# Requesting the inverse blocks of a pair's first chunk at the second step of a slot

## The chip, the cores and the metric

The kernel runs on one core of a Trainium2 chip. The metric is the device time of one execution in microseconds, as the median of several runs; lower is better.

## What is computed

The reference is a linear recurrence followed by a feed-forward layer. In the first part, for each of 4 batches and 8 heads, a 40 by 40 state runs over 768 time steps; in the second part the outputs of all heads are put side by side as 3072 tokens of 320 numbers.

```python
for t in range(S):                                   # per batch and head
    y[t] = einsum('d,de->e', r[t], state)
    Sa = einsum('de,e->d', state, a[t])
    state = state * w[t][None, :] - einsum('d,e->de', Sa, b[t]) + einsum('d,e->de', v[t], k[t])
h = maximum(x @ w_in, 0)                             # x: (3072, 320), w_in: (320, 2048)
out = (h * h) @ w_out                                # w_out: (2048, 320)
```

All of it is float32.

## The kernel before

The time axis is cut into six chunks of 128 steps, which with four batches gives 24 pieces of work, called chunks 0 to 23 here (`order`, line 138, runs over the batches fastest). Inside a chunk the recurrence is solved as a triangular system, so each chunk needs an inverse of a unit triangular matrix for every head. The matrices are made early (`early`, line 360), stored to DRAM (`kept_q`, `kept_m`, `kept_n`, `kept_d`), and inverted on GpSimd by forward substitution in eleven units of 1, 1, 2, 2, 2, 2, 2, 2, 4, 4 and 2 chunks (`solving`, line 456). `take` (line 442) loads a unit's matrices into `half_n`; the last instruction of `solving` writes the inverses to `kept_t`.

For units 0 to 7 (chunks 0 to 13, "fine" in the code) only the inverses of 32 by 32 diagonal blocks are computed on GpSimd. The generator `inverses` (line 495) puts them together to 64 by 64 inverses `T` in four stages, each ending at a `yield`:

1. the requests on the SyncE queue: two transfers of `blocks` from `kept_t` (line 508), one of `N` from `kept_n` (line 489), two of `joins`, a part of the tile `spares`, from `kept_m` (line 493);
2. a transpose of `blocks` on VectorE (line 515) and two scaled copies of `blocks` into `T` on ScalarE (line 517);
3. 16 small matmuls with `joins` on TensorE and two copies out of PSUM (line 527);
4. 16 small matmuls with `blocks` and two copies into `T` (line 534).

Chunks 0 to 6 are woven into an opening whose order is written out by hand. From chunk 7 on each chunk has a slot, `sorted_slot` (line 973), which interleaves four things in an order written out by hand: the chain of chunk i (`ch`: the triangular solve, the output, the state), the preparation of chunk i+1 (called j), the early part of one or two later chunks (`one`, `two`), and the feed-forward layer of earlier tokens (`second`). There is no scheduler: the order in which the code issues is the order on each engine's queue. `tick` runs at the end of each `step` and issues delayed stores.

The preparation of chunk j includes the four stages of `inverses` for j. Where chunk j has the same unit as chunk j-1 (chunks 9, 11, 13, the second of a pair) or its request stood in the opening (chunk 8), stage 1 has been issued before slot j-1 begins: `loads`, line 956, does it at the end of the slot before. These chunks are `early_join`. The first chunk of a pair, which among the slots with fine units is chunk 10 (slot 9) and chunk 12 (slot 11), is not.

The slot calls `join()`, which advances `inverses` by one stage, at two places for fine chunks (lines 999 and 1006), once more at line 1011 if the chunk is not `early_join`, and runs what is left at line 1021. So in slots 9 and 11 stage 1 stands at line 999, stage 2 at 1006, stage 3 at 1011 and stage 4 at 1021; in slots 7, 8, 10 and 12 stage 2 stands at 999, stage 3 at 1006 and stage 4 at 1021.

At line 992, `on(one)` starts the early part of a later chunk, which first requests that chunk's successor's w, b and a (`load_early`, line 149). At line 993 `fetch_next` requests r for chunk j+1; at line 1008 it requests v. The store of 128 output rows is issued by `make_quarter` two ticks after its copy (line 789). All of these are on the SyncE queue. The built program gives the transfers on this queue eight semaphores in turn, so that a request may have to wait until the one eight places ahead of it has landed.

Of the kernel before, what the change touches and what calls it, by code (L numbers as in the profile page):

```python
# [17 lines left out]
def kernel(  # L18
# [82 lines left out]
    def tick():  # L101
        for entry in line:
            entry[0] -= 1
        while line and line[0][0] <= 0:
            line.pop(0)[1]()
# [389 lines left out]
    def inverses(i, g, queue=nc.sync, own_n=True):  # L495
        bb, c = order[i]
        u = unit_of[i]
        kept = kept_t[u][:, i - units[u][0]]
        g["T"] = T = new("T", [128, H, HC], 2)
        if u >= FINE:  # L500
            for col in range(classes(u)):
                queue.dma_start(out=T[col::classes(u)], in_=kept[col].rearrange("h f j t -> (f j) h t"))
        else:


            blocks = new("blocks", [128, H, Q], 1)
            for col in range(classes(u)):
                queue.dma_start(out=blocks[col::classes(u)], in_=kept[col].rearrange("h f k j t -> (f k j) h t"))  # L508
        if own_n:
            arrive(i, g, queue)  # L510
        if u >= FINE:
            return
        yield
        upper_ = spare("turned", i)
        nc.vector.transpose(upper_.rearrange("p h t -> p (h t)"), blocks.rearrange("p h t -> p (h t)"))
        for n in range(2):
            nc.scalar.activation(T[:, :, n * Q:(n + 1) * Q], blocks, Act.Copy, scale=which[:, n:n + 1])
        yield
        small = lambda: psum(ps_w)[:, :H * Q].rearrange("p (h t) -> p h t", h=H)
        p_ = small()  # L520
        mv = spare("mv", i)
        ends_ = [(slice(half * HC, half * HC + Q), slice(half * HC + Q, (half + 1) * HC)) for half in range(2)]
        for h in range(H):
            for one, two in ends_:
                mm(p_[two, h], g["joins"][one, h], upper_[one, h], True)
        for one, two in ends_:
            nc.scalar.copy(mv[two], p_[two])
        yield
        p_ = small()
        for h in range(H):  # L530
            for one, two in ends_:
                mm(p_[one, h], mv[two, h], blocks[two, h], True)
        for one, two in ends_:
            nc.scalar.copy(T[one, :, Q:], p_[one])
        yield
# [61 lines left out]
    def begin(i, g):  # L597
        g["x"] = loaded.pop(i)
        g["up"], g["aT"] = g["dec"][:, UP], g["dec"][:, A_, :, :C]
# [206 lines left out]
    def run(gen):  # L806
        for _ in gen:
            tick()
# [13 lines left out]
    def prepare(i, g=None, apart=False, steps=0):  # L822
        gen = early(i, g, apart)
        for _ in range(steps):
            next(gen)
            yield
        if i + 1 < len(order) and i + 1 not in early_loaded:
            load_early(i + 1)
        yield from gen
# [63 lines left out]
    def begin_chain(j, n_=None):  # L893
        n_ = decays_of(j)
        n_["chain"] = chain(j, n_)
        next(n_["chain"])
# [54 lines left out]
    def fetch_next(i, *names):  # L951
        if i < len(order):
            to = ready[i]["x"] if "x" in ready.get(i, {}) else loaded.setdefault(i, {})
            to.update({nm: fetch(nm, {"k": k, "b": b, "r": r, "v": v}[nm], i) for nm in names if nm not in to})

    def loads(j):
        if j < len(order):
            n = ready.setdefault(j, {})
            n["dec"] = kept_here[j % 2]
            nc.sync.dma_start(out=n["dec"][:USED], in_=kept_e[j])  # L960
            fetch_next(j, "k", "b")
            if soon(j) and j > B:
                n["joining"] = inverses(j, n)
                next(n["joining"], None)

    def step(*what):
        for w_ in what:
            w_()
        tick()
# [3 lines left out]
    def sorted_slot(i, g, ch):  # L973
        j = i + 1
        more = j < len(order)
        n = ready.setdefault(j, {}) if more else None
        made = [prepare(m_, apart=True) for m_ in ahead.get(i, ())]
        one, two = (made + [iter(()), iter(())])[:2]
        if j in inversions:
            n["joining"] = inversions.pop(j)  # L980
        early_join = more and "joining" in n
        joining = n.pop("joining") if early_join else inverses(j, n) if more else iter(())
        fine = more and unit_of[j] < FINE
        join = on(joining)
        of = lambda fn: (lambda: fn(j, n)) if more else (lambda: None)

        if more and "x" in n:
            n.update(up=n["dec"][:, UP], aT=n["dec"][:, A_, :, :C])
        elif more:
            begin(j, n)  # L990
        step(second.make_quarter)
        step(of(turn_rv), on(one), on(one))
        fetch_next(j + 1, "r")
        step(second.make_quarter)
        step(on(ch), of(decay_state))
        step(of(make_rv), second.thirds)
        step(on(ch), on(one))
        if fine:
            join()
        step(second.whole)  # L1000
        step(on(ch))
        step(on(one), of(turn_k))
        step(on(one), on(ch), of(turn_down))
        step(on(ch), of(scale_kb))
        if fine:
            join()
        step(on(ch), of(make_a), second.thirds, on(one))
        fetch_next(j + 1, "v")
        step(of(turn_state), second.square, second.whole, on(two))
        if not early_join:  # L1010
            join()
        run(ch)
        if more:
            begin_chain(j, n)
        loads(j + 1)
        step(second.square, second.make_quarter, on(two), on(two))
        if i in ahead and len(ahead[i]) > 1:
            step(on(two), on(two))
        step(second.make_quarter, on(two))
        for gen in (one, two, joining):  # L1020
            run(gen)

    for i in range(LAID, len(order)):
        tc.no_sync_barrier()
        g = ready.pop(i)
        opening[0] = 0
        ch = g["chain"]
        done.update(ahead.get(i, ()))
        sorted_slot(i, g, ch)
        while unit < len(units) and all(m_ in done for m_ in range(len(order)) if unit_of[m_] == unit):  # L1030
            flush()
            take(unit, own)
            solve(unit)
            unit += 1
# [32 lines left out]
```

## Time and profile before

| | us |
|---|---|
| median of three runs | 962.63 |
| lowest, highest run | 957.42, 964.86 |
| the profiled execution | 964.61 |
| its span, first to last instruction | 962.8 |

| engine | busy us | share of the span |
|---|---|---|
| TensorE matmul | 912.0 | 95% |
| TensorE weight load | 723.9 | 75% |
| GpSimd | 531.3 | 55% |
| VectorE | 452.6 | 47% |
| ScalarE | 287.2 | 30% |

The profile shows one execution. Times in it count from the start of the span; the 1.8 us between the span and the execution's own time lie outside the first and the last instruction. TensorE is busy nearly all the time, so a change is felt where TensorE stands still or runs at a lower granted clock, and only there. The slots from chunk 7 on can be told apart by the first chain matmuls of a slot (`ps_c<-xr,T`); slot 9 reaches from 417.14 to 459.60 us by this mark, slot 11 from 493.88 to 528.44 us.

### The profile page before, as it was taken

What the parts mean: (1) busy time and instruction counts of PE and PEld (TensorE: products, weight loads), DVE (VectorE), ACT (ScalarE), POOL (GpSimd) and SP (SyncE); (2) the same over time, 40 slices, a digit from 0 to 9 for tenths busy, and PEclk for the clock granted to TensorE, in tenths of its full rate; (3) what the DMA queues carried; (4) which work ended last, traced back from release to release, by engine and by line L of the source; (5) the groups of instructions that cost most, each with busy time, mean ns of one, the idle gap of its engine ahead of it and who ended that gap; (6) DMA issues with size and microseconds to landing.
All of it is one profiled execution on the core that took longest, in us unless ns stands there. A gap on an engine that the chain in (4) does not pass through costs nothing.

```text
span 962.8 us, 22650 instructions
## 1 busy us (share of the span) xinstructions
PE 912.0 (95%) x9156; PEld 723.9 (75%) x9156; DVE 452.6 (47%) x1064; ACT 287.2 (30%) x735; POOL 531.3 (55%) x1001
## 2 busy tenths in 40 slices
PE   5978989789999999989999999999999999999998
PEld 4645656568787887877888888887888888887776
DVE  4516647687863455533654543644234323231111
ACT  3123234544432343333423322222222222222111
POOL 4788508356008686319999849999768860000000
PEclk8889888798899999998999999999999999999999
DMA  9589767776875677893655695515554253120000
GB/s 110 113 160 175 155 129 139 170 177 126 163 116 131 114 159 138 168 170 82 114 90 99 116 191 110 110 24 85 120 112 78 44 107 69 42 42 9 14 14 14
DMA packets 253222, 103.36 MB, mean 107 GB/s; under 512 B 234143, under 2 KB 240159, under 8 KB 251967
## 3 DMA queue, kind: packets, MB, share of 16 engines
q1 hardware_dynamic: 246869, 83.43, 48.1%
q0 software_dynamic: 3600, 16.25, 6.8%
q10 hardware_dynamic: 2650, 2.25, 0.9%
q8 instruction: 72, 1.18, 0.6%
q14 instruction: 31, 0.25, 0.1%
HBM read 69.00 MB, written 30.92 MB: 104 GB/s over the span
## 4 chain that ended last, share of the span: by engine, by line
PE 80%; DVE 8%; ACT 3%; POOL 2%; issue 2%; SPq 2%; DMA 2%; DVEq 0%; POOLq 0%; ACTq 0%
PE ps_f L87 40%; PE ps_w L87 16%; PE ps_c L87 13%; PE ps_w L331 5%; PE ps_f L264 3%; PE ps_c L666 1%; PE ps_c L593 1%; SPq L508 1%; POOL half_p L477 1%; POOL half_t L479 1%; PE ps_w L577 1%; DMA blocks<-kept_t 1%; SPq L146 1%; DVE w_out L291 1%; DVE RX L347 1%
## 5 line engine op out<-in xcount | busy, mean ns | idle before, releaser
L477 POOL TENSOR_TENSOR half_p<-half_n,half_t 128x126 f32<-128x126 f32 (+44 forms) x437 | 232.0, 531 | 78.5 <-DMA half_n<-kept_d 23.0
L479 POOL TENSOR_TENSOR half_t<-half_t,half_p 128x126 f32<-128x126 f32 (+44 forms) x437 | 249.0, 570 | 34.2
L87 PE MATMUL ps_f<-w_out,hid 128*128 128x320 f32 x768 | 218.7, 436 | 0.0
L87 PEld LDWEIGHTS ps_f<-w_out,hid 128*128 128x128 f32 x768 | 142.0, 190 | 54.0 <-issue 0.2
L87 PE MATMUL ps_f<-tokens,w_in 128*128 128x256 f32 x672 | 160.1, 393 | 0.0
L87 PEld LDWEIGHTS ps_f<-tokens,w_in 128*128 128x128 f32 x672 | 128.4, 196 | 19.8 <-issue 2.0
L764 DVE TENSOR_TENSOR hid<-hid 128x512 f32<-128x512 f32 x96 | 82.3, 895 | 50.1 <-ACT hid L757 49.8
L757 ACT ACTIVATE hid<-ps_f 128x512 f32<-128x512 f32 x84 | 50.0, 597 | 88.2 <-PE ps_f L87 88.1
L264 PE MATMUL ps_f<-ident 128*128 128x512 f32 (+2 forms) x148 | 71.9, 625 | 0.0
L347 DVE TENSOR_TENSOR RV<-ps_w,upper 128x512 f32<-128x512 f32 x48 | 30.9, 685 | 50.3 <-PE ps_w L87 50.0
L451 POOL DMA_DIRECT2D half_n<-kept_q x18 | 9.4, 528 | 79.6 <-DMA kept_q<-N 51.6
L692 DVE TENSOR_TENSOR tokens<-ps_c,dec 128x512 f32<-128x512 f32 x24 | 16.6, 690 | 78.0 <-PE ps_c L87 78.0
L372 DVE TENSOR_TENSOR_SCAN decay<-ps_w,ones 128x64 f32<-128x64 f32 x88 | 23.6, 268 | 59.6 <-PE ps_w L331 59.4
L87 PE MATMUL ps_f<-tokens,w_third 64*128 64x256 f32 x336 | 47.4, 392 | 2.5 <-ACT hid L757 2.5
L264 PEld LDWEIGHTS ps_f<-ident 128*128 128x128 f32 x148 | 29.3, 215 | 26.7 <-issue 25.7
L347 DVE TENSOR_TENSOR RX<-ps_w,upper 128x512 f32<-128x512 f32 x48 | 30.8, 683 | 37.2 <-PE ps_w L87 36.8
L543 DVE TENSOR_TENSOR kvT<-ps_w,dec 128x512 f32<-128x512 f32 x24 | 16.5, 687 | 62.9 <-ACT minus_x L653 35.3
L87 PEld LDWEIGHTS ps_c<-xr,T 64*64 64x64 f32 x768 | 28.7, 143 | 20.4 <-issue 16.8
L398 ACT COPY N<-ps_w 128x256 f32<-128x256 f32 x48 | 17.7, 368 | 80.2 <-PE ps_w L87 54.8
L565 DVE TENSOR_TENSOR f<-end,dec 128x4 f32<-128x4 f32 x20 | 7.0, 348 | 64.7 <-DMA dec<-kept_e 64.7
L555 ACT COPY rT<-ps_w 128x512 f32<-128x512 f32 x24 | 14.0, 585 | 77.6 <-PE ps_w L331 77.5
L87 PE MATMUL ps_c<-xr,T 64*64 64x40 f32 x768 | 34.8, 237 | 1.4 <-ACT xr L660 0.8
(146 smaller groups left out, 1429.5 us busy)
## 6 DMA issues: line engine op xcount, KB each, us to landing
dec<-kept_e SPq DMA_DIRECT2D x22, 633.8 KB
kept_e<-decay SPq DMA_DIRECT2D x19, 633.8 KB
in_w<-in_w_dram SPq DMA_DIRECT2D x24, 160.0 KB
in_b<-in_b_dram SPq DMA_DIRECT2D x24, 160.0 KB
in_ab<-in_a_dram SPq DMA_DIRECT2D x24, 160.0 KB
in_r<-in_r_dram SPq DMA_DIRECT2D x24, 160.0 KB
in_v<-in_v_dram SPq DMA_DIRECT2D x24, 160.0 KB
out_dram<-o SPq DMA_DIRECT2D x24, 160.0 KB
```

The source lines that it names most:

```text
L87: nc.tensor.matmul(o, l_, r_, start=start, stop=True, skip_group_check=True)
L264: nc.tensor.matmul(fill_bank[:, :n * 128], ident, ident.unsqueeze(1).to_broadcast([128, n, 128]), start=True, stop=True, skip_group_check= ...
L331: nc.tensor.transpose(p_[:, q * 128:(q + 1) * 128], pair(x_, q), ident)
L347: nc.vector.tensor_tensor(t_, p_, over4(upper), Alu.mult)
L372: nc.vector.tensor_tensor_scan(up[:, q, MID + 1:C + 1], wT[:, q, MID:], ones, 1.0, Alu.mult, Alu.mult)
L398: nc.scalar.copy(plain, p_[:, ::2].rearrange("s h (f t) -> s f h t", f=2))
L477: nc.gpsimd.tensor_tensor(p_, part[:, at:at + m_].unsqueeze(1).to_broadcast([128, n, m_]), t3[:, :n, s:s + 1].to_broadcast([128, n, m_]), ...
L479: nc.gpsimd.tensor_tensor(t3[:, :n, s + 1:], t3[:, :n, s + 1:], p_, Alu.subtract)
L543: nc.vector.tensor_tensor(kT, kT_, down[:, :, 1:C + 1], Alu.mult)
L692: nc.vector.tensor_tensor(t_, y_, g["up"][:, :, :C], Alu.mult)
L757: nc.scalar.activation(h_, p_.rearrange("p f t -> p (f t)"), Act.Relu)
L764: nc.vector.tensor_tensor(h_, h_, h_, Alu.mult)
```

## The change

For fine chunks that are not `early_join`, one more `join()` is called right after the slot's first step, and the one at line 1011 is left out for them.

```diff
         step(second.make_quarter)
+        if fine and not early_join:
+            join()
         step(of(turn_rv), on(one), on(one))
         fetch_next(j + 1, "r")
...
         step(of(turn_state), second.square, second.whole, on(two))
-        if not early_join:
+        if not early_join and not fine:
             join()
```

This holds for chunks 10 and 12, thus for slots 9 and 11. In these two, stage 1 moves ahead of the slot's second step: on the SyncE queue its five requests stand in front of the requests for w, b and a of a later chunk, the request for r and the store of the output. (The request for v stood behind them before as well.) Stage 2 moves from line 1006 to line 999, and stage 3 from 1011 to 1006. The number of instructions on each engine stays the same, and no other slot changes.

The order of the instructions after the change, in slots 9 and 11, against before:

- SyncE: `blocks` twice, `N`, `spares` twice, then w, b, a, r, the output's store; before: w, b, a, r, the store, then the five.
- VectorE: the transpose of `blocks` comes directly after the scans of a later chunk (lines 380, 381) and ahead of `kvT`, `bT` and the scaling of k and b; before it came after them, directly ahead of `RX`.
- ScalarE: the two copies of `blocks` into `T` come ahead of the two ReLU copies `hid` and of the copy `minus_x`; before they came after `xnT`.
- TensorE: the 16 matmuls with `joins` come ahead of the products for `RX`; before they came ahead of the chain's `ps_c<-RV`.

The first `blocks` request waits on one more thing: the buffer `blocks` exists once, so TensorE must have done the last stage of the chunk before, the matmuls `ps_w<-blocks,spares`.

## The prediction

> **What bounds the kernel now.** I read the busy shares first (TensorE 95%), then the chain of waits that ended last. From 257 us on the chain is nearly all TensorE; the largest break in it is in slot 9:
>
> ```profile
> 424.97 0.29 ACT minus_x L653
> 425.26 1.54 SPq L110
> ...
> 426.89 1.90 SPq L508
> ...
> 428.85 5.36 DMA blocks<-kept_t
> ...
> 434.30 0.45 DVE spares L515
> 434.74 0.59 DVE RX L347
> ...
> 435.38 2.67 PE ps_w L87 x16
> ```
>
> Columns: start, length, what. So TensorE at 435.38 waits for VectorE's `RX`, that for the transpose of `blocks`, that for the transfer, that for its issue. Then I cut the table of busy times by slot (8 to 13) and slot 9 by its stall (length, then busy times of PE, weight loads, DVE, ACT, POOL, the granted clock, DMA share, GB/s):
>
> ```profile
> 379.95:417.14 37.19, 36.75 (x441) 31.05 (x440) 20.84 (x63) 13.63 (x39) 12.13 (x33) 1.00 0.85 161
> 417.14:459.60 42.46, 38.07 (x414) 31.63 (x413) 16.34 (x39) 11.85 (x31) 28.63 (x42) 0.92 0.65 121
> 459.60:493.88 34.28, 34.28 (x414) 28.77 (x413) 20.62 (x42) 11.54 (x31) 32.11 (x28) 1.00 0.71 119
> 493.88:528.44 34.56, 34.56 (x413) 29.11 (x412) 18.04 (x39) 11.65 (x31) 32.34 (x29) 1.00 0.38 79
> 528.44:562.72 34.28, 34.28 (x414) 28.77 (x413) 17.13 (x43) 11.54 (x31) 26.52 (x40) 1.00 0.81 155
> ...
> 430.99:435.38 4.39, 0.01 (x1) 0.01 (x1) 1.08 (x3) 0.91 (x2) 3.37 (x10) 0.92 0.79 171
> 435.38:441.51 6.13, 6.13 (x27) 5.26 (x28) 3.31 (x5) 2.68 (x9) 5.50 (x9) 0.50 0.27 79
> ```
>
> Slot 9 has as many matmuls as slots 10 and 12 (414) and takes 8.18 us more than either. It stands still for 4.39 us, then runs 6.13 us at a clock of 0.50. Half of these 6.13 us is 3.07 us, to which come some 0.37 us already inside the idle stretch and the slower start (clock 0.92 there), and 0.28 us that slot 11, equal in form and undisturbed, also takes over 34.28: 4.39 + 3.07 + 0.28 = 7.74, the other 0.44 us I leave as rounding of modelled ends. The difference between whole slots, 8.18, is what I use.
>
> Why is `blocks` late? The SyncE queue:
>
> ```profile
> 417.19 0.58 SPq L146 DMA_DIRECT2D in_w<-in_w_dram  x1
> 417.86 0.64 SPq L146 DMA_DIRECT2D in_ab<-in_b_dram  x1
> 418.59 0.55 SPq L146 DMA_DIRECT2D in_ab<-in_a_dram  x1
> 419.23 0.71 SPq L146 DMA_DIRECT2D in_r<-in_r_dram  x1
> 420.03 6.77 SPq L110 DMA_DIRECT2D out_dram<-o  x1
> 426.89 3.21 SPq L508 DMA_DIRECT2D blocks<-kept_t  x2
> ...
> 418.59 1.03 POOL L451 DMA_DIRECT2D half_n<-kept_d  x2 [23.79 <-DMA kept_d<-N]
> ```
>
> The store of the output sits in issue for 6.77 us, though its input was copied at 417.67; in slot 11 the same store takes 0.36 us. At 418.59 GpSimd requests unit 8, two transfers of 768 KB. The trace's packet records give the rest: the 128 packets of 12288 bytes of these transfers start at 420.0 and the last ends by 429.7, about 1 us each; the SyncE queue's packets of 160 bytes start at 1350 per us from 419 to 420, at 16 to 17 per us from 420.5 to 423.5, about 580 come through between 423.75 and 425.25 (between GpSimd's two transfers), and then 12 to 18 per us until 427.75. Four loads of 1024 packets each had been put in front; a little over half was through at 420.25. So `blocks`, behind them, lands at 434.2. VectorE and ScalarE had waited 5.45 and 7.17 us for it.
>
> **What the Trainium skill says.** "DMA: Bandwidth & Descriptors", section on queues, rings and completion order: each DMA engine goes round robin, packet by packet, between the queues that have work. The trace agrees: with 16 engines and 1 us per large packet, one small packet between two large ones gives the 16 per us. "Perfetto Trace Analysis", section on the HWDGE DMA instruction: the issue's recorded window begins when its semaphores are satisfied and holds the generation of descriptors[...]. So the 6.77 us are a full buffer and not a wait for an engine; the "ACT minus_x" put in the chain ahead of it is a coincidence. "TensorE: Matmul & The Clock Gate", part on the clock gate: an idle window of about 3.4 us puts the array at half clock until it has been busy for another. The trace agrees: 4.39 us idle, then a clock of 0.50.
>
> **The change part by part.** It only moves instructions, in slots 9 and 11.
>
> *Slot 9, requests.* SyncE is free at 417.14, after the store of `kept_n`. The new wait, for TensorE's last read of `blocks`, is over: those matmuls ran at 410.70 to 411.4. The inverses of this unit were stored at 359.24, and the transfers eight places ahead had landed by 417.85, or, for the later ones, before their turn. With the issue times of slot 11's five (0.65, some 0.7, 0.62, 0.6, 0.6), they start at 417.19, 417.85, 418.5, 419.15 and 419.75. From issue to landing the two `blocks` transfers took 3.0 and 2.7 us in slot 11 (494.89 to 497.92, 495.59 to 498.33); hence 420.2 and 420.6. First packets came 1.3 us after issue, and 512 packets take 0.4 us at 1350 per us: those of the second end near 419.6, 0.4 us before the first large packet. `N` (64 packets) falls on the edge, the two `joins` transfers (512 packets) inside the stretch at 16 per us; the gap at 423.75 to 425.25 lets 580 through, so I put their landing at 425.5 to 426.
>
> *Slot 9, who waits.* VectorE reaches the transpose at 422.3, where it then has 3.81 us without work: 0.45 us, free. ScalarE is done with `xr` at 421.05 and with nothing until 422.31: the two copies, 0.91 us, fit if `blocks` lands by 421.4; up to 422.5 only `hid` would shift, and from 423.1 on the chain's `minus_x` and TensorE's transposes of it at 425.89. TensorE wants `joins` in front of the `RX` products, at 10.61 us into the slot as in slot 10 (470.21 - 459.60), so at 427.75: about 2 us of slack. Then slot 9 has the order of slot 10 and should take its 34.28 us: -8.18 us.
>
> *Slot 9, what is pushed back.* The loads of w, b, a, r and the store move back by five requests, most of them behind GpSimd's burst. The sum of the packets is unchanged, so all should be through at about 434 as before. In slot 9 itself none of them is read; r is transposed first at 456.04, w at 456.91, minus 8.2 at the new pace: 14 us of cover. If this cover were gone, TensorE would stop at the next slot's start for as long as r was late. Behind them stand the store of decays, the stores of N for unit 9, v, the moves of tokens and the next slot's decays. The moves wait for VectorE's `tokens` at 447, 439 at the new pace, so a queue that is empty by 437 costs nothing.
>
> *Slot 11.* Here the new wait bites: the last read of `blocks` in slot 10 is at 487.44 to 488.06, while SyncE is free for the next request at 484.3. It stands 3.7 us with w, b, a, r and the store behind it; before, the same 3.6 us went into issuing w (484.36, 3.58 us). `blocks` then lands near 491.5, and is wanted from 497.8. No large burst is near (DMA share 0.38). The slot becomes 34.28 instead of 34.56: -0.28 us, which might as well be zero.
>
> *Afterwards.* From slot 10 on TensorE had no idle time in slots 10 to 13, so nothing hides the gain, but GpSimd's solving keeps its times, and TensorE comes 8.4 us earlier. The stores of unit 8, 9 and 10's inverses land at 560.6, 698.0 and 792.6; the first reads of them are requested at 582.2, 698.0 (here the queue already waits) and 814.2. For unit 9 the transfer lands at 706.8 and is used at 721.1, 712.7 at the new pace: 6 us of slack remain. GpSimd's request for unit 9 at 554.97 would meet slot 13 from its start instead of the end of slot 12; the loads that it delayed there (a, issued over 10.19 us) are then ahead of it.
>
> Sum: -8.18 - 0.28 = -8.46. Against the profiled execution's own time, 964.61, that is 956.15; it lies 1.98 above the median, so at the median 962.63 - 8.46 = 954.2, or -0.88%. About 1% is what a measurement of this kernel can tell from no change (the three runs spread over 7.4 us), so even the full gain is just inside it.
>
> **The rivals.**
>
> *A, the stall goes wholly (0.60):* 954.2; with the spread of the runs, 950 to 957.5.
>
> *B, a shorter wait takes its place (0.22):* `joins` has only the gap in GpSimd's burst to get through. If an engine's share is not through then, it comes with the burst's end at 429 or so, and TensorE stands about 2 us ahead of the `RX` products, too short for the clock; if `blocks`' last packets are caught, ScalarE holds `minus_x` until 425.3 + 2.65 and TensorE stands another 2 us. For it: packets inside the burst at 16 per us. Against: 512 packets, and 580 came through. 2 to 4 us are lost: 956.2 to 958.2.
>
> *C, no gain to be seen (0.10):* the stall is only in this execution (the lowest run, 957.42, may have none), or GpSimd's fixed pace takes the gain back, unit 9 being the tightest. Against: 6 us of slack there. 959 to 963.
>
> *D, slower (0.08):* the two copies and the transpose now stand in front of `minus_x` on ScalarE and of `kvT` on VectorE. If the burst catches `blocks` and it lands with the rest at 434.2, the chain stops at 425.89 and resumes 2.65 us (copies, two `hid`, `minus_x`) after the landing, at 436.85: 10.96 us idle, then 3.4 to 6.8 us for the clock, against 8.18 won: 968.8 to 972.2. From a landing at 428 on it is slower than before. Against: 0.4 us of margin before the burst, and the gap.
>
> **How the numbers follow.** Predicted is A: 954.2. The range reaches from A's lower end, 949.5, over B to most of C, 962.0; D and a rest of A and C are left out. Faster by over 1% means under 953.0: nearly half of A, a little of B, 0.30. Slower by over 1% means over 972.3: the upper end of D and runs of it, 0.06. The rest, 0.64, is within 1%.
>
> **What would show it.** Right: in slot 9 five requests ahead of `in_w`, `blocks` landing near 420.5, no idle TensorE near 431, a clock of 1.00 throughout, a slot of 34.3 us; slot 11 within 0.3 us; all later slots as long as before. The store of the output may still sit long in issue, now unnoticed. Wrong: an idle TensorE ahead of the `RX` products (B), ahead of `ps_c<-ident,minus_x` (D), or at slot 18's `ps_c<-xr,T` (C).

## The result, and the profile after

| | us |
|---|---|
| after, median of 20 runs | 958.21 (952.52 to 963.97) |
| before on the same chip, median of 20 runs | 961.64 (956.35 to 966.83) |
| ratio, 95% interval | 0.9966 [0.9948, 0.9984] |
| the profiled execution after | 959.58, span 957.7 |
| the profiled execution before | 964.61, span 962.8 |

The change gains 3.4 us at the median, where 8.46 were predicted. So less than half of the expected gain came. Measured twice more on other chips the same kernel gave 0.9918 [0.9893, 0.9944] and 0.9952 [0.9933, 0.9971]. How much the stall differs between executions of the same kernel is shown below.

First the table by slots for the kernel after, in the columns of before: slots 8, 9, 10 and 11, then the stall in slot 9 and the stretch at a lower clock that follows it.

```profile
380.56:417.75 37.19, 36.74 (x441) 31.06 (x441) 20.85 (x63) 13.75 (x39) 12.43 (x34) 1.00 0.88 166
417.75:454.71 36.96, 36.20 (x414) 30.19 (x413) 15.87 (x39) 11.55 (x31) 26.45 (x39) 0.95 0.74 135
454.71:488.98 34.27, 34.27 (x413) 28.76 (x412) 19.78 (x43) 11.55 (x31) 32.05 (x29) 1.00 0.64 115
488.98:523.26 34.28, 34.28 (x414) 28.76 (x413) 18.77 (x40) 11.55 (x31) 32.08 (x29) 1.00 0.49 85
...
428.43:429.13 0.70, 0.00 (x0) 0.03 (x1) 0.70 (x3) 0.00 (x0) 0.29 (x1) 1.00 1.37 93
431.90:435.30 3.40, 3.40 (x28) 2.96 (x24) 3.40 (x6) 0.00 (x0) 3.01 (x6) 0.51 0.86 254
```

Slot 9 fell from 42.46 to 36.96 us, not to 34.28. What is left over 34.28 is 2.68 us: 0.70 us in which TensorE has nothing to do, half of 3.40 us at half clock (1.7 us), and some 0.28 us that are not told apart. Slot 11 went from 34.56 to 34.28. All other slots from 7 on kept their lengths to 0.04 us; what lies ahead of slot 9 took 0.61 us longer in this execution. So 0.61 - 5.50 - 0.29 is the -5.2 us between the two profiled spans.

The SyncE queue of the kernel after (start, length, what), and below it GpSimd's request of unit 8 from the same view of its own queue:

```profile
416.60 1.37 SPq L508 DMA_DIRECT2D blocks<-kept_t  x2
418.02 0.62 SPq L489 DMA_DIRECT2D N<-kept_n  x1
418.69 1.25 SPq L493 DMA_DIRECT2D spares<-kept_m  x2
419.98 0.65 SPq L146 DMA_DIRECT2D in_w<-in_w_dram  x1
...
422.79 5.60 SPq L146 DMA_DIRECT2D in_ab<-in_a_dram  x1
...
429.76 0.87 SPq L110 DMA_DIRECT2D out_dram<-o  x1
```

```profile
418.12 1.04 POOL L451 DMA_DIRECT2D half_n<-kept_d  x2 [22.33 <-DMA kept_n<-N]
```

The `blocks` requests are out before GpSimd's burst and, by the trace's landing times, are in at 419.03 and 419.62. The two `spares` requests (that is `joins`) go out at 418.69 and 419.33 and land at 429.00 and 429.36, ten microseconds later. The long issue has moved from the output's store (6.77 us before) to the load of a (5.60 us). (The view puts GpSimd's request down to the store of `kept_n`. That store landed at 418.28, after the request; the last store of `kept_d`, which the request reads, landed at 417.39.)

What that does to TensorE, in its order of time (in brackets: idle before, and what ended it; the trace counts 32 instructions for the 16 matmuls with `joins`):

```profile
427.37 1.06 PE L87 MATMUL ps_c<-rT,sd 128*128 128x128 f32 x8
429.13 0.96 PE L87 MATMUL ps_w<-spares 32*32 32x32 f32 x32 [0.70 <-DMA spares<-kept_m]
...
431.91 1.88 PE L87 MATMUL ps_f<-tokens,w_third 64*128 64x256 f32 x8
433.58 1.92 PE L87 MATMUL ps_w<-decay,bT 40*128 40x128 f32 x16
```

and the chain of waits of this stretch, which before ran through `blocks`:

```profile
418.69 0.59 SPq L493
...
419.33 10.03 DMA spares<-kept_m
...
429.40 2.68 PE ps_w L87 x62
```

Followed back from TensorE, the chain goes to the transfer of `joins`, and from there along the SyncE queue and over ScalarE's making of `N` to a load of decays (`dec<-kept_e`, 405.16 to 411.46). The stall of before was not removed wholly: a shorter wait took its place, and the clock fell although the wait was short.

### The profile page after: what moved, and what is told of

Its sections match the earlier page's. It is cut to its first block, busy times and chain, and to the rows that moved or that the text cites. A ratio compares the mean times of both kernels' runs of the same rounds, so it can differ in the third digit from the quotient of the medians.

```text
span 957.7 us, 22644 instructions
## 1 busy us (share of the span) xinstructions
PE 913.9 (95%) x9156; PEld 725.4 (76%) x9156; DVE 451.0 (47%) x1064; ACT 287.4 (30%) x735; POOL 531.9 (56%) x1001
## 4 chain that ended last, share of the span: by engine, by line
PE 72%; DMA 4%; DVE 2%; ACT 2%; SPq 1%; issue 0%; ACTq 0%; DVEq 0%
PE ps_f L87 40%; PE ps_w L87 13%; PE ps_c L87 12%; PE ps_w L331 4%; DMA dec<-kept_e 2%; DMA spares<-kept_m 2%; PE ps_c L593 1%; PE ps_c L666 1%; PE ps_w L577 1%; DMA hid<-in_moe_w_out_dram 1%; ACT N L401 0%; SPq L508 0%; DMA kept_t<-half_t 0%; SPq L146 0%; SPq L110 0%
## 5 line engine op out<-in xcount | busy, mean ns | idle before, releaser
L87 PEld LDWEIGHTS ps_f<-tokens,w_third 64*128 64x128 f32 x336 | 31.0, 192 | 6.5 <-ACT hid L757 3.7
```

What stands on the lines that cost most here:

```text
L87: nc.tensor.matmul(o, l_, r_, start=start, stop=True, skip_group_check=True)
```

## The experiments

My theory after this reading: what is left is the wait of stage 3 (the 16 matmuls with `joins`) for a transfer that only lands with the end of GpSimd's burst; the early requests themselves are good. Rivals: the early stage 2 costs on VectorE and ScalarE; `N` in front of `joins` is what uses up the gap in the burst; the rest is the position of the burst in that execution.

**late_use: the requests early, the use where it was.** Stage 1 stays at the slot's second step, stages 2 to 4 go back to their places of before (the edit is shown against the changed kernel, from its line 1000 on).

```diff
-        if fine:
+        if fine and early_join:
             join()
...
-        if not early_join and not fine:
+        if not early_join:
             join()
```

> The changed kernel's order on the SyncE queue, with stages 2 to 4 left where the kernel before had them. Theory 1 (what is left of the stall is the joins transfers caught in GpSimd's burst, wanted too early by the moved stage 3): blocks lands near 419.6 us, ahead of the transpose at 428.8; joins lands near 429 and is wanted some 18.7 us into the slot, near 436; TensorE doesn't stop, no half clock, slot 9 takes 34.6 us instead of 37.0 (changed) and 42.5 (before), slot 11 34.6: some 2.1 us faster than the changed kernel, 5.5 us and more below the kernel before (0.994). Rival (the early request delays what stands behind it, r and the store, and that costs): slot 9 stays at 37 us or above, or slot 10 grows over 34.3, and the time stays at that of the changed kernel (0.9966).

953.57 us, ratio 0.9894 [0.9870, 0.9919], a larger gain than the 0.994 expected. Slot 9, and the matmuls with `joins` in it:

```profile
413.20:447.76 34.56, 34.56 (x413) 29.11 (x412) 15.69 (x38) 11.66 (x31) 24.08 (x37) 1.00 0.82 144
```

```profile
431.90 0.69 PE L87 MATMUL ps_w<-spares 32*32 32x32 f32 x32
```

The `joins` transfers land at 424.62 and 424.92, 10.5 and 10.2 us after their issue, as late as in the changed kernel. But they are wanted only 18.7 us into the slot instead of 10.7, so 7 us are to spare: no idle time, a clock of 1.00. A second measurement of the same kernel on another chip:

> The kernel with the requests at the slot's second step and the use of blocks and joins where it was before, once more, beside stage3_late on one chip. If its gain (0.989 in the first measurement) belongs to the kernel: 0.987 to 0.992 again, slot 9 at 34.3 to 34.6 us. If that was a lucky position of GpSimd's burst (it came 0.17 us into the slot there): slot 9 of 36 us or more here wherever the burst comes 1 us or more into the slot.

954.48 us, ratio 0.9924 [0.9897, 0.9951], just outside the expected 0.987 to 0.992; slot 9 took 34.57 us again. GpSimd's request came 0.23 us into the slot there, so this run did not test the kernel against a late burst; the next one did.

**stage3_late: only stage 3 put back.** The changed kernel, with stage 2 left early.

```diff
         step(on(ch), of(scale_kb))
-        if fine:
+        if fine and early_join:
             join()
...
-        if not early_join and not fine:
+        if not early_join:
             join()
```

> The changed kernel with one difference: the 16 matmuls with joins (stage 3) stand where they stood before the change, after the output and the state's parts, in slots 9 and 11; the requests at the slot's second step and the early stage 2 (transpose and copies of blocks) stay. My theory: what is left of the stall in the changed kernel is the wait of these 16 matmuls alone, for joins that land near 429 to 429.7 with the end of GpSimd's burst. Used later, they find joins there: TensorE has no idle time in slot 9, the slot takes 34.3 to 34.6 us, and the ratio to before is 0.989 to 0.991. Rival: the early stage 2 costs as well (VectorE's transpose ahead of kvT, ScalarE's copies ahead of minus_x); then slot 9 stays at 36 us or more and the ratio at 0.993 or above, as in the changed kernel.

954.90 us, ratio 0.9919 [0.9894, 0.9943]: the slot as expected, the ratio a little above the 0.989 to 0.991 named and under the 0.993 of the rival.

```profile
415.39:449.96 34.57, 34.57 (x413) 29.12 (x412) 15.70 (x38) 11.65 (x31) 22.69 (x35) 1.00 0.80 146
```

```profile
434.10 0.69 PE L87 MATMUL ps_w<-spares 32*32 32x32 f32 x32
```

Here GpSimd's request came 1.86 us into the slot, nearly as late as in the worst run of the changed kernel below, `joins` landed at 428.31 and 428.62, and TensorE still never waited, since it wanted them at 434.10. This is the cleanest test: same requests, same early transpose and copies, only the 16 matmuls later, and the remaining stall is gone. The early stage 2 costs nothing in this slot; the early stage 3 is what meets the burst.

**joins_first: the burst turned on `blocks`.** The changed kernel with the order `joins`, `blocks`, `N` in stage 1.

```diff
-            if unit_of[i] < FINE:
+            if unit_of[i] < FINE and "joins" not in g:
...
+            if i in (10, 12):
+                g["joins"] = spare("joins", i)
+                for half in range(2):
+                    queue.dma_start(out=g["joins"][half * HC:half * HC + Q], in_=kept_m[i][half, :, :, Q:])
```

> The changed kernel with the order of the five requests turned for chunks 10 and 12: joins twice, blocks twice, N last. Theory 1: joins issued at 416.6 lands near 419, blocks at 418 to 418.6 lands near 420.5, just ahead of the burst or with its tail in it; N lands at 430, but nobody reads it before slot 10. If blocks is in time, slot 9 takes 34.3 us, 2.7 us less than in the changed kernel, ratio to before about 0.993. If the tail of blocks is caught, ScalarE holds minus_x, and TensorE stops at the transposes of minus_x for up to 2 us: slot 9 at 36 to 38. Rival (not the joins but something else held TensorE at 429): slot 9 stays at 37.0 with the idle time at the same place.

960.40 us, ratio 0.9981 [0.9963, 0.9999]; slot 9 took 42.08 us, nearly as long as before and longer than the 36 to 38 us expected for a `blocks` caught by the burst. `joins` landed at 414.50 and 415.23, the second `blocks` transfer at 425.10, 10.7 us after issue. TensorE then stands where the prediction's slower rival put it, at the transposes of `minus_x`, held on ScalarE behind the copies of `blocks`:

```profile
427.43 1.21 PE L670 MATMUL ps_c<-ident,minus_x 128*128 128x128 f32 x4 [5.43 <-ACT minus_x L657]
```

So the mechanism of that rival exists. Here it was worth 5.43 us of idle time and 6.8 us at half clock, of which 2.2 us fell into the idle time. In the changed kernel `blocks` had landed by 419.62 in each of its three profiled executions, so it did not happen.

**joins_mid: `N` behind `joins`.** Order `blocks`, `joins`, `N`.

```diff
-            queue.dma_start(out=g["N"], in_=kept_n[i])
+            if i not in (10, 12):
+                queue.dma_start(out=g["N"], in_=kept_n[i])
...
+            if i in (10, 12):
+                queue.dma_start(out=g["N"], in_=kept_n[i])
```

> The changed kernel with N asked for last: blocks twice, joins twice, N, for chunks 10 and 12. Refined theory 1: in the changed kernel the 64 packets of 2048 bytes of N stood ahead of joins and used up the gap between GpSimd's two transfers, so that joins came only with the burst's end. With N last, the 512 packets of 128 bytes of joins pass in the gap (some 580 small packets did in the kernel before): joins lands 3 to 4 us earlier, about 6.5 us after its issue instead of 10.3, TensorE does not stop, slot 9 takes 34.3 us, the ratio to before is near 0.991. Rival (the gap is too short for joins whatever stands ahead of it): joins lands with the burst's end again, slot 9 stays between 34.8 and 37.

957.27 us, ratio 0.9931 [0.9913, 0.9950]; slot 9 took 39.64 us, above what either theory or rival had allowed. The theory that `N` alone kept `joins` from the gap fell:

```profile
424.75 0.24 PE L87 MATMUL ps_w<-spares 32*32 32x32 f32 x2
426.96 1.03 PE L87 MATMUL ps_w<-spares 32*32 32x32 f32 x30 [1.96 <-DMA spares<-kept_m]
```

Two matmuls run at 424.75, the other 30 wait for the second transfer, which landed at 426.91 with the burst's end. By the packet records exactly the 256 packets of the first transfer came through until the gap closed, and none of the second.

**after_again and after_third: the changed kernel once more**, on two other chips.

> The changed kernel once more, for a second profile and for times beside the three others. Theory 1: slot 9 again at about 37.0 us with an idle TensorE of 0.5 to 2 us ahead of the joins matmuls, ratio to before near 0.9966. Rival (the length of the stall varies by some us from run to run, which would bring 3.4 us in the medians against 5.0 in the profiled executions): slot 9 anywhere from 35 to 40 us.

> The changed kernel a third time. Theory 1: slot 9 between 34.8 and 38 us, set by where the end of the burst falls against the place of the joins matmuls at 10.6 us into the slot, and by whether the wait brings a stretch of half clock (3.4 us, costing 1.7); ratio to before between 0.992 and 0.9966. Rival: slot 9 always near one value, and the two ratios measured so far differ by something else.

The ratios are 0.9918 and 0.9952, given above. Slot 9 of after_again and its matmuls with `joins`; then the same of after_third:

```profile
418.29:453.13 34.84, 34.52 (x414) 28.88 (x413) 15.86 (x38) 11.53 (x31) 24.24 (x37) 1.00 0.77 138
```

```profile
429.29 0.88 PE L87 MATMUL ps_w<-spares 32*32 32x32 f32 x32 [0.32 <-DVE decay L388]
```

```profile
415.85:456.63 40.78, 37.76 (x413) 31.78 (x413) 16.39 (x38) 11.54 (x31) 27.86 (x41) 0.92 0.71 128
```

```profile
429.55 0.89 PE L87 MATMUL ps_w<-spares 32*32 32x32 f32 x32 [3.02 <-DMA spares<-kept_m]
```

(In after_again the first `joins` transfer landed at 429.15 and the scaling at L388 ended at 429.20, so there the two ended the wait together.) In the same program slot 9 took 34.84, 36.96 and 40.78 us; so the rival named for after_again, a stall that differs by some us between runs, holds, and after_third lies outside the 34.8 to 38 us expected. One number orders the three: how far into the slot GpSimd's request of unit 8 came.

| run | GpSimd's request, us into slot 9 | last `joins` lands, us into the slot | TensorE is free for it at | idle | at half clock | slot 9 |
|---|---|---|---|---|---|---|
| after_again | -0.61 | 11.14 | 10.68 | 0.32 | none | 34.84 |
| after | 0.37 | 11.61 | 10.68 | 0.70 | 3.4 | 36.96 |
| after_third | 1.94 | 13.85 | 10.68 | 3.02 | 6.8 | 40.78 |
| stage3_late | 1.86 | 13.23 | 18.71 | none | none | 34.57 |

The landing follows the request by 11.2 to 11.9 us in each. The request itself comes 0.73 or 0.74 us after the landing of the last store of `kept_d`, which it reads (417.39 and 418.12 in the kernel after, 416.94 and 417.68 in after_again, 417.05 and 417.79 in after_third), and those stores landed between 1.35 us ahead of the slot's start and 1.20 us behind it. What moves the stores against the slot from run to run was not pursued. Nor do these profiles explain the three ratios: each shows one execution, and 0.9966 goes with a slot of 36.96 us but 0.9952 with 40.78. Why the medians differ stays open.

**before_again: the kernel before once more**, for the size of its own stall.

> The kernel before once more, for a second profile. Theory 1: slot 9 near 42.5 us again, with blocks landing with the rest of the backlog. Rival: the stall differs by some us between runs of the same kernel; then slot 9 is under 40 us here, and this is why the medians differ less than the two profiled executions.

One run, 958.99 us beside a median of 963.56 for the others on that chip. Slot 9 took 41.75 us against 42.46, with 3.03 us idle, ended by VectorE's `RX`, and 6.8 us at half clock. So the stall of before is there in both profiled executions and nearly the same in length, as expected.

**burst_later: the burst away, the old order kept.** The kernel before, with unit 8's request moved to the SyncE queue at the end of slot 9 (the condition inside `all` is left out below).

```diff
-        while unit < len(units) and all(...):
+        while unit < len(units) and (unit != 8 or i >= 9) and all(...):
...
-            take(unit, own)
+            take(unit, [nc.sync] if unit == 8 else own)
```

> The kernel before, with GpSimd's request for unit 8 put on the SyncE queue at the end of slot 9, behind the requests for chunk 11; the rest in the order of before. Theory 1 (the burst, not the order of the requests, makes blocks late): w, b, a, r, the store and blocks all flow at full rate, blocks lands near 424, 4 us ahead of the transpose at 428.8, slot 9 takes 34.6 us although blocks is asked for late. Rival (the five requests ahead of blocks are enough to delay it): blocks lands after 429 and slot 9 takes 37 us or more. Unit 8's inverses come some 40 us later and are then late for chunk 14, so a new stall near 590 us is expected and the whole time says nothing.

982.94 us, one run. The total is not the point: GpSimd solves unit 8 late, so that TensorE waits 14.16 us for the inverses at the end of slot 13 (47.36 us) and begins slot 14 at half clock (37.51 us). Slot 9 is:

```profile
413.42:447.99 34.57, 34.57 (x414) 29.12 (x413) 14.47 (x38) 11.65 (x31) 0.00 (x0) 1.00 0.58 102
```

With requests in the order of before, `blocks` lands at 420.44 and 420.69, 3.1 and 2.7 us after issue, and slot 9 loses nothing. The place of the requests on the queue was never the fault by itself; the burst was. (GpSimd computes nothing in this slot either. That is not the cause: in slot 11 of the kernel before it was busy for 32.34 us, no burst ran, and the two transfers took 3.0 and 2.7 us.) The burst was taken away from the old order only; no run did so for the changed kernel.

**at_loads: the requests a slot earlier.** The kernel before, with stage 1 of chunks 10 and 12 issued at the end of the slot before, as for the other fine chunks; this makes them `early_join`, with the early use of stages 2 and 3.

```diff
-    soon = lambda i: i < 2 * B or unit_of[i - 1] == unit_of[i]
+    soon = lambda i: i < 2 * B or unit_of[i - 1] == unit_of[i] or i in (10, 12)
```

> The kernel before, with stage 1 of chunks 10 and 12 requested at the end of the slot before, as for chunks 9, 11 and 13. Theory 1: all five land before 417 us, well ahead of GpSimd's burst, slots 9 and 11 get the order of slot 10 and take 34.3 us each: ratio to before about 0.992. The five requests stand in front of the stores for unit 8, so that the burst itself comes up to 3 us later. Rival: the first request waits for TensorE's last read of blocks and holds these stores and the next loads; slot 8 or slot 10 grows, and the ratio is 0.996 or more.

953.35 us, ratio 0.9897 [0.9870, 0.9924].

```profile
417.70:451.97 34.27, 34.27 (x413) 28.76 (x412) 14.90 (x39) 11.54 (x31) 17.25 (x30) 1.00 0.82 160
```

The requests, out from 411.99 on, were 11 us ahead of GpSimd's, which itself came later here, at 423.37, because the stores of `kept_d` now stand behind them. The last `joins` landed at 417.63, just after the 417 us expected and still 10.7 us ahead of its use. Early use is harmless where the data are early.

Which is best? late_use (0.9894, 0.9924), stage3_late (0.9919) and at_loads (0.9897) all beat the kernel before. late_use and at_loads ran on one chip with after_again: 953.57 and 953.35 us against 955.99, with intervals of the ratios that overlap, so their medians alone do not show that they beat the changed kernel. Slot 9 does: 34.27 to 34.57 us in the four profiled executions of the three variants, 34.84 to 40.78 in the three of the changed kernel.

## Why the prediction was right and wrong

*What bound the kernel: right.* The break in slot 9 came from `blocks` behind the burst; burst_later shows the burst as the cause, and the three variants show that the slot without the stall takes 34.27 to 34.57 us.

*Requests and landing of `blocks`: right, even early.* Predicted 420.2 and 420.6; landed 419.03 and 419.62, in a slot that began 0.6 us later. That they got ahead of the burst was not luck by these runs: in all eight executions with the requests at the second step the first of the five went out 1.33 to 1.53 us ahead of GpSimd's request, because both follow the same stores on the SyncE queue. Two transfers got through on this lead, and the third was always caught: `N` here, `joins` in joins_mid, `blocks` in joins_first.

*How the queues share the engines: right for the alternation, not for its size.* The section of the Trainium skill that the prediction cites ("DMA: Bandwidth & Descriptors", queues, rings and completion order) lets an engine take a packet of some 9 to 17 descriptors from one queue before it turns to the other. In the trace of the kernel before, one small packet came for each large one, 8 or 9 against 8 to 10 in every half microsecond from 421 to 423.5. The prediction rightly counted with this measured rate, but said that the trace agrees.

*Landing of `joins`: this step failed.* "The gap at 423.75 to 425.25 lets 580 through, so I put their landing at 425.5 to 426", against 429.00 and 429.36. Two things were wrong in it. The 580 packets of before were of a single transfer of 1024 that stood at the head of the queue; I read them as a capacity that any packets may use. In the changed kernel the head was `N`, whose 64 packets of 2048 bytes came at 14 to 19 per us in the first execution, and `joins` behind it had to wait. Nor would another order have helped: in joins_mid just the 256 packets of the first `joins` transfer were through, in joins_first just the 512 of the first `blocks` transfer, and the next transfer came with the burst's end. And I took the burst of one execution as fixed to the slot, where it moves by 2.5 us against it.

*"About 2 us of slack": therefore wrong.* The time at which TensorE wants `joins` was right (10.61 us into the slot predicted, 10.68 measured), but the transfer is 0.5 to 3.2 us later than that. That is rival B in mechanism and place. I gave it 0.22 on the strength of a count that did not carry over. That its 956.2 to 958.2 us end where 958.21 was measured is luck: B left 4.4 to 6.4 us of gain on a median of 962.63, and 3.4 us came, on a median of 961.64. B had no cost for the clock.

*The clock: wrong.* I called a wait of 2 us "too short for the clock". An idle time of 0.70 us was followed by 3.4 us at half clock, and 3.02 us by 6.8 us. In after_third that is 3.4 us more lost, more than the wait itself. For rival D the prediction erred the other way: it put 3.4 to 6.8 us for the clock, which are the lengths of such stretches, where its own sum for the stall of before counts half as lost (3.07 of 6.13 us). And the 0.37 us that it names there for half clock within the idle stretch cost nothing, because TensorE stood still.

*What is pushed back: right.* w, b, a and r landed at 430.19, 431.41, 432.59 and 434.18 ("about 434"), and slots 9 and 10 never waited for them. The long issue went to the load of a instead of the store, unnoticed.

*Slot 11: right.* SyncE stood for 4.2 us, until 483.28, for the last read of `blocks` (3.7 us predicted); `blocks` landed at 485.76 and 486.32, and the slot became 0.28 or 0.29 us shorter as said.

*Afterwards: right in effect.* No later slot gave anything back. GpSimd did not keep its times, though: its request for unit 9 moved from 554.97 to 552.32.

*The sum.* -8.18 for slot 9 was mis-sized. Three profiled executions of the changed kernel give 37.5 us on average for it, two of before 42.1 us, so -4.6 us; with slot 11 -4.9 us or a ratio of 0.9949, where the three measurements average 0.9945. With five profiles in all this agreement is a check of the size and no more. The term that failed is thus the wait for `joins`, put at nothing with 2 us to spare: it was 0.32 to 3.02 us, and up to 3.4 us for the clock came on top.

## What to carry to other kernels

A request moved ahead of a burst must have all its parts ahead of it: count to the last transfer that the consumer waits for, not to the first, and do not count on gaps in the burst. Here two requests got ahead, whichever they were. If a part cannot get ahead, leave its consumer where it was; early requests and late use took the stall away wholly here, at a slot of 34.57 us against 34.27 for early use of early data. Before trusting a slack of 2 us, see from a second profile how far the other queue's burst moves against the work.

## What was not expected of the hardware

- Half clock after short gaps. The Trainium skill, "TensorE: Matmul & The Clock Gate", part 1, speaks of an idle window of about 3.4 us ahead of half clock, and its closing table of gaps over about 3 us. The measurements differ: in the slots looked at here a stretch of 3.4 us at half clock followed an idle time of 0.70 us, and stretches of 6.8 us idle times of 1.96, 3.02, 3.03, 4.39 and 5.43 us; after 0.32 us (after_again) there was none, nor after the 0.44 or 0.45 us that TensorE stands still in slot 8 of all twelve traces. The lengths, 3.4 and twice that, agree with the page's window. The clock's records tell more: within each of the twelve traces all changes of the clock lie whole multiples of 3.413 us apart, so they fall on a fixed grid of windows. Idle time within a window does not decide alone. In the kernel after, the window from 428.54 to 431.95 held 0.65 us of idle time and all the matmuls with `joins`, and half clock followed. In after_third, 0.75 us of the 3.02 lay in the window from 423.87 to 427.28, beside larger matmuls only, and the next window still ran at full clock. Whether the small matmuls count for less than large ones was not tested.
- In the gap between GpSimd's two transfers only the transfer at the head of SyncE's queue came through. It was so with 64 packets (`N` in after_again and after_third), with 256 (joins_mid) and with 512 (joins_first); why the next one does not follow stays open.
